# Layer 0's increments of x gathered in 128 columns, a ring of 20 KB instead of 28 KB, and 8 KB more of K kept for layer 1

## The chip, the core and the metric

One NeuronCore of one Trainium2 chip runs the whole program. Five engines work side by side and meet at semaphores: TensorE (PE, with its weight loads shown apart as PEld), VectorE (DVE), ScalarE (ACT), GpSimd (POOL) and SyncE (SP), which here only issues the DMAs. The data comes from HBM over 16 DMA engines. The metric is the device time of one execution in microseconds (us), the median of the runs. "KB" below is always KB for each of the 128 partitions: 1 KB is 256 float32 numbers of a row, and 128 KB of memory over all partitions.

## The reference

Two layers of a decoder for four sequences with one token each, in float32. x has shape 4 x 512. Both layers use the same weights and the same cache.

```python
def _A_ref(x, k_cache, v_cache, wq, wo):       # 32 query heads, 8 heads of K and V, 4096 positions, Dh 128
    q = (x @ wq).reshape(B, Sq, Hq, Dh).transpose(0, 2, 1, 3)
    scores = jnp.einsum("bhqd,bhkd->bhqk", q, k) * (Dh ** -0.5)
    o = jnp.einsum("bhqk,bhkd->bhqd", _softmax(scores), v)
    return o.transpose(0, 2, 1, 3).reshape(B, Sq, Hq * Dh) @ wo

def _B_ref(x, w1, w3, w2):                     # 512 -> 1792 -> 512
    h = _silu(x @ w1) * (x @ w3)
    return h @ w2

x = x + _A_ref(_layernorm(x), k_cache, v_cache, wq, wo)
x = x + _B_ref(_layernorm(x), w1, w3, w2)
x = x + _A_ref(_layernorm(x), k_cache, v_cache, wq, wo)
x = x + _B_ref(_layernorm(x), w1, w3, w2)
```

K and V hold 64 KB for each of the 8 heads of K and V, wq and wo 64 KB each, w1, w3 and w2 28 KB each.

## The kernel before

**Memory.** One tile, `arena`, of 218 KB is handed out by the program itself. `WQ` (0 to 64) holds wq for all heads, `WO` (64 to 128) first takes K and V of layer 0 and then wo, `KEPT` (128 to 192) at the end of layer 0 holds V of the last head (`TURN`, head 7), which layer 1 uses first. From 192 to 216 lies the ring of the transition between the layers, `PT` (214, 2 KB) is the turned softmax weights, `FIRST` (216, 2 KB) holds a piece of K.

**The list of loads.** `plan` is a list of all loads in the order in which they are issued. `pump()` goes through it and issues each load on SP's queue as soon as a place is free; it stops at the first that has none. `done` and `vacate` give a place back behind the last instruction that reads it, and call `pump` again. SP carries the list out in order: a load whose place is still being read holds up all loads behind it. With `at` a load goes to a given place, otherwise `take` looks for the lowest free one.

**The order of work.** Layer 0 goes through heads 0 to 7, layer 1 through 7 to 0. For each head, `scores` multiplies q with 8 blocks of K (8 KB each), `factors`, `exponents` and `turn_p` make the softmax weights, and `weigh` multiplies with V of the head before. After head 7 of layer 0 comes the transition: `project_o` for all 8 heads, `collect` (adds the increment to x), `feed_forward` of layer 0 (w1, w3, w2), `collect` again, `project_q` of layer 1, and `scores` of head 7.

**The ring.** In the transition 84 KB of w1, w3 and w2 and the first pieces of layer 1's K pass through 7 places of 4 KB: the first 4 KB of `WO` (its part of wo is kept in PSUM meanwhile, `stash` and `restore`) and 24 KB from 192. The pieces are w1a, w3a (4 KB, 4 of each: the first 256 of each 448 columns), w1b, w3b (3 KB, 4 of each), w2 (4 KB, 7), and seven halves of K blocks (4 KB). `feed_forward` uses them in the order w1a, w3a, w1b, w3b 0 and 1, w2 0 (`down(0)`), w3b 2 and 3, w2 1 to 6; L124 to L140 list the loads in that same order.

**What is kept of K.** While layer 0 scores the first block of head 7, ACT copies 2 KB of it to PSUM (`keptk`, L417) and POOL 2 KB to `first` (L418). Layer 1 begins its scores with these (L406), so the first half block need not be loaded again. Blocks 0 to 3 (`SPLIT`) of head 7 come to layer 1 in halves, blocks 4 to 7 whole (8 KB).

**The increments of x.** `whole` and `pair` (L484 to L496) multiply with 512 or 256 columns; the four parts of the sum lie in 32-row groups of `x_ps` over all 512 columns. `collect` copies them to SBUF (DVE 256 columns, ACT 256), adds the four groups and turns them to 128 rows with four products against `rows` (L335), and adds the mean with one more (L338). `idle` and `busy` are products without use, which keep TensorE at work.

**Layer 1's q.** `q_product` (L348) multiplies with the 8 KB of wq of one head and gives them back with `vacate`; the next whole K blocks of layer 1 are loaded there.

Of the kernel before, what the change touches and what calls it, by code (L numbers as in the profile page):

```python
# [10 lines left out]
ALU = mybir.AluOpType  # L11
# [3 lines left out]
LAYERS = 2  # L15
# [18 lines left out]
SPLIT = 4  # L34
# [4 lines left out]
def tile_decode_layers(ctx: ExitStack, tc: tile.TileContext, x, kt, v, wq, wo, w1, w3, w2, w2s, out):  # L39
# [12 lines left out]
    PT, FIRST = ARENA - 4, ARENA - 2  # L52
    free = [(WO, PT - WO)]
    ring = {"to": 0}

    def take(n, at=None):
        if at is not None and at < WO:
            return at
        for i, (lo, size) in enumerate(free):
            if at is None and state["next"] > ring["to"]:  # L60

                end = min(lo + size, PT)
                if lo < WO + 4 and end > WO:
                    if WO - lo >= n:
                        end = WO
                    else:
                        lo = WO + 4
                if end - lo < n:
                    continue
                a = lo  # L70
                lo, size = free[i]
            else:
                a = lo if at is None else at
            if lo <= a and a + n <= lo + size:
                free[i:i + 1] = [(p, s) for p, s in ((lo, a - lo), (a + n, lo + size - a - n)) if s]
                return a
        return None
# [46 lines left out]
    RING = KEPT + 64  # L124
    slots = [WO] + [RING + 4 * i for i in (5, 4, 3, 2, 1, 0)]
    for i in range(4):
        piece("w1a", i, (slots[6], slots[1], slots[2], slots[3])[i])
    for i in range(4):
        piece("w3a", i, (slots[4], slots[5], slots[0], slots[6])[i])
    for i in range(4):  # L130
        piece("w1b", i, RING + 21 - 3 * i)
# [140 lines left out]
    first = arena[:, FIRST * KB:]  # L272
    pT = arena[:, PT * KB:FIRST * KB].rearrange("p (i r) -> p i r", i=NI)
# [51 lines left out]

    def collect():
# [14 lines left out]

        def mean():
            m = misc()
            nc.tensor.matmul(m[:, 0, :], both.broadcast_to([P, P]), off[:, 0, :], start=True, stop=True)  # L344
            nc.vector.tensor_tensor(mu, mu, m[:, 0, :], op=ALU.subtract)
        return mean

    def q_product(layer, g, ps, j, first, last):  # L348
        w = loaded("wq", 0, g).rearrange("p (k n) -> p k n", k=KC)
        lo = PAD - B * j  # L350
        for k in range(KC):
            nc.tensor.matmul(ps[32 * k:32 * k + 32, :], xpad[:, 32 * k + lo:32 * k + lo + 32], w[:, k, :], start=first, stop=last)  # L352
        if layer:
            vacate("wq", 0, g)
# [45 lines left out]
    def scores(layer, g, pieces=iter(())):  # L400
        for blk in range(NB):
            split = layer == 1 and g == TURN and blk < SPLIT
            keys = [("half", layer, 2 * blk + i) for i in range(2)] if split else [("k", layer, g, blk)]
            if split and blk == 0:
                for b, k in enumerate((p, first)):
                    nc.tensor.matmul(s_ps[32 * b:32 * b + 32, :], qpad[:, 32 * b + PAD:32 * b + PAD + 32], k, start=True, stop=False)  # L406
                del keys[0]
            lo = PAD - REP * blk
            for i, key in enumerate(keys):
# [6 lines left out]
            if g == TURN and blk == 0 and not layer:  # L416
                nc.scalar.copy(keptk, loaded(*keys[0])[:, 0:BK])  # L417
                nc.gpsimd.tensor_copy(first, loaded(*keys[0])[:, BK:2 * BK])  # L418
            for key in keys:
                done(*key)  # L420
# [71 lines left out]
    def whole(i, left, w, first):  # L492

        for n in range(2):
            r = 32 * (2 * i + n)
            nc.tensor.matmul(x_ps[r:r + B, :], left(2 * i + n), w(n), start=first, stop=False)  # L496
# [10 lines left out]
    def project_o(layer, g, first=False, last=False):  # L507
        for i in range(2):
# [3 lines left out]
            if last:  # L512
                pair(i, lambda h: oT(layer, g)[:, h, :], lambda j: w[:, j, :], False, last and i == 1)
            else:
                whole(i, lambda h: oT(layer, g)[:, h, :], lambda j: w[:, j, :], first)
# [5 lines left out]
    def feed_forward(layer, mean):  # L521
# [32 lines left out]
        def columns(rows, m, w, last=False):  # L554
            for k in range(KC):
                nc.tensor.matmul(x_ps[32 * k:32 * k + B, 0:P], hT[rows, m, :], w[rows, k * P:(k + 1) * P],  # L556
                                 start=False, stop=last)

        def few(lo, hi):
            for u in range(lo, hi):  # L560
                at = (where["few"] + 2 * u) * KB
                columns(slice(0, FEW), WT + u, arena[:, at:at + 2 * KB])
# [51 lines left out]
        for m in range(1, WT):  # L614
            columns(slice(0, P), m, loaded("w2", layer, m), m == WT - 1)
# [10 lines left out]
    for layer in range(LAYERS):  # L626
# [38 lines left out]
        feed_forward(layer, collect())  # L665
        if layer < LAYERS - 1:
            mean = collect()
# [43 lines left out]
```

## Time and profile before

| | |
|---|---|
| median of 3 runs | 705.38 us (705.28 to 705.43) |
| the profiled execution | 705.23 us, its span 703.4 us, so 1.8 us lie around the span |
| TensorE clock granted | 0.808 of full speed on average |
| busy: PE, DVE, ACT, POOL | 409.9, 85.2, 38.0 and 3.5 us |
| read from HBM | 298.33 MB, 424 GB/s over the span |
| transition, first o product to first score product of layer 1 | 344.98 to 390.12 us |

A group of instructions stands on one row with its line, engine, operation, tiles written and read, and count; "x8" of a matrix product in float32 is four products, since each is made of two instructions. In the timeline the first column is the start, the second the time up to the end of the group, and the brackets tell the idle time before it and what ended it. The DMA rows give the busy share of the 16 DMA engines in tenths and the GB/s in equal slices.

### The profile page before, as it was taken

The numbers are of one execution on the slowest core, as the hardware profiler recorded it, in microseconds if no ns is written. First come the engines' busy times: TensorE is split into PE (matmuls) and PEld (weight loads), VectorE is DVE, ScalarE is ACT, GpSimd is POOL, SyncE is SP. The second block draws the span as 40 slices with busy tenths as digits, with TensorE's granted clock in tenths as the row PEclk, the third lists the DMA queues.
The fourth block names the chain that finished last, engine by engine and source line by source line (L and its number), as shares of the span: only waits on it lengthen the run. The fifth ranks groups of instructions, "written<-read, shape, count | busy, mean of one in ns | idle before, by whom it ended". The sixth has DMA issues, their size and how long they took to land. (4 is left out here: it accounts for less than half of the span.)

```text
span 703.4 us, 7079 instructions
## 1 busy us (share of the span) xinstructions
PE 409.9 (58%) x3172; PEld 136.4 (19%) x3172; DVE 85.2 (12%) x291; ACT 38.0 (5%) x87; POOL 3.5 (0%) x11
## 2 busy tenths in 40 slices
PE   2555454456456454538888894365563545467687
PEld 1112011112111111112233331011120111122234
DVE  2001010101001010101111111020000101010111
ACT  0000000000000000101001000000000000000100
POOL 0000000000000000000000000000000000000000
PEclk9986776767777776878999997588787878688899
DMA  9999999999999999999999999999999999999996
GB/s 418 432 403 466 422 418 426 462 415 432 433 444 418 440 444 421 421 428 427 414 404 403 420 431 461 429 425 418 459 425 425 437 444 418 432 433 420 424 424 277
DMA packets 13605, 298.85 MB, mean 425 GB/s; under 512 B 1655, under 2 KB 1783, under 8 KB 6263
## 3 DMA queue, kind: packets, MB, share of 16 engines
q1 hardware_dynamic: 13440, 298.39, 99.1%
q8 instruction: 25, 0.41, 0.2%
q14 instruction: 5, 0.04, 0.0%
q10 hardware_dynamic: 135, 0.01, 0.0%
HBM read 298.33 MB, written 0.07 MB: 424 GB/s over the span
## 5 line engine op out<-in xcount | busy, mean ns | idle before, releaser
L461 PE MATMUL o_ps<-arena 128*32 128x512 f32 x1024 | 146.8, 723 | 144.4 <-DMA arena<-in_v 131.0
L414 PE MATMUL s_ps<-arena,qpad 128*32 128x512 f32 x1020 | 150.1, 742 | 90.1 <-DMA arena<-in_kt 90.1
L461 PEld LDWEIGHTS o_ps<-arena 128*32 128x32 f32 x1024 | 37.4, 130 | 251.9 <-issue 222.4
L414 PEld LDWEIGHTS s_ps<-arena,qpad 128*32 128x32 f32 x1020 | 39.5, 132 | 183.7 <-issue 176.6
L470 DVE SCALAR_TENSOR_TENSOR p<-o_ps,parts,p 128x512 f32<-128x512 f32 x16 | 12.0, 751 | 266.9 <-PE o_ps L461 266.9
L424 DVE TENSOR_REDUCE top<-s_ps 128x1 f32<-128x512 f32 x16 | 11.1, 691 | 196.9 <-PE s_ps L414 196.9
L468 ACT ACTIVATE p<-o_ps,parts 128x512 f32<-128x512 f32 x16 | 11.0, 687 | 189.9 <-PE o_ps L461 182.3
L292 PE MATMUL m_ps<-ident,rows 128*32 128x256 f32 (+1 forms) x84 | 20.9, 352 | 0.0
L352 PE MATMUL o_ps<-arena,xpad 128*32 128x512 f32 x112 | 15.4, 672 | 7.9 <-DMA arena<-in_wq 7.9
L447 PE MATMUL t_ps<-ident,p 128*128 128x128 f32 x64 | 11.4, 305 | 13.5 <-ACT p L441 13.5
L474 PE MATMUL t_ps<-ident,p 128*128 128x128 f32 x64 | 10.5, 287 | 13.9 <-DVE p L470 13.8
L496 PE MATMUL x_ps<-arena,qT 128*4 128x512 f32 x112 | 13.8, 592 | 5.4 <-DVE qT L482 3.6
L434 ACT ACTIVATE f<-d 128x1 f32<-128x1 f32 x16 | 3.2, 203 | 252.8 <-DVE d L432 252.8
L441 ACT ACTIVATE p<-s_ps,top 128x512 f32<-128x512 f32 x16 | 10.9, 684 | 77.3 <-PE t_ps L474 77.3
L448 DVE COPY arena<-t_ps 128x512 f32<-128x512 f32 x16 | 11.1, 691 | 9.7 <-PE t_ps L447 9.7
L474 PEld LDWEIGHTS t_ps<-ident,p 128*128 128x128 f32 x64 | 6.7, 140 | 28.2 <-DVE p L470 28.2
L447 PEld LDWEIGHTS t_ps<-ident,p 128*128 128x128 f32 x64 | 7.3, 150 | 22.2 <-ACT p L441 19.2
L292 PEld LDWEIGHTS m_ps<-ident,rows 128*32 128x32 f32 x84 | 9.0, 110 | 9.0 <-issue 3.5
L529 PE MATMUL o_ps<-arena,xpad 128*32 128x192 f32 (+1 forms) x128 | 8.1, 360 | 1.0 <-DMA arena<-in_w 0.9
L529 PE MATMUL s_ps<-arena,xpad 128*32 128x192 f32 (+1 forms) x128 | 7.9, 359 | 1.3 <-DMA arena<-in_w 1.3
L489 PE MATMUL x_ps<-arena,qT 128*4 128x256 f32 x88 | 6.6, 379 | 2.4 <-DMA arena<-in_w 1.7
L352 PEld LDWEIGHTS o_ps<-arena,xpad 128*32 128x32 f32 x112 | 3.6, 121 | 17.2 <-DMA arena<-in_wq 8.8
(107 smaller groups left out, 144.2 us busy)
## 6 DMA issues: line engine op xcount, KB each, us to landing
arena<-in_v SPq DMA_DIRECT2D x4, 4096.0 KB, 38.4
arena<-in_w SPq DMA_DIRECT2D x17, 512.0 KB, 13.4
arena<-in_kt SPq DMA_DIRECT2D x8, 1024.0 KB, 11.3
arena<-in_kt SPq DMA_DIRECT2D x2, 4096.0 KB, 18.1
arena<-in_wq SPq DMA_DIRECT2D x1, 7168.0 KB, 39.8
arena<-in_v SPq DMA_DIRECT2D x3, 2048.0 KB, 31.8
arena<-in_wo SPq DMA_DIRECT2D x1, 4096.0 KB
arena<-in_kt SPq DMA_DIRECT2D x2, 2048.0 KB
```

Source lines behind the costliest of these rows:

```text
L292: nc.tensor.matmul(m_ps[0:32, (4 - w) * P:], rows, ident.unsqueeze(1).broadcast_to([P, w, P]), start=True, stop=True)
L352: nc.tensor.matmul(ps[32 * k:32 * k + 32, :], xpad[:, 32 * k + lo:32 * k + lo + 32], w[:, k, :], start=first, stop=last)
L414: nc.tensor.matmul(s_ps[32 * b:32 * b + 32, :], qpad[:, 32 * b + lo:32 * b + lo + 32], k[:, j, :], start=(blk == 0), stop=(blk == NB - 1))
L424: nc.vector.tensor_reduce(top[:, 0:1], s_ps, axis=AX.X, op=ALU.max, negate=True)
L447: nc.tensor.transpose(t_ps[:, i, :], p[:, i * P:(i + 1) * P], ident)
L448: nc.vector.tensor_copy(pT.rearrange("p i r -> p (i r)"), t_ps.rearrange("p i r -> p (i r)"))
L461: nc.tensor.matmul(o_ps[32 * b:32 * b + 32, :], pT[:, i, 32 * b:32 * b + 32], w[:, b, :], start=(i == 0), stop=(i == NI - 1))
L468: nc.scalar.activation(p, o_ps, AF.Copy, scale=st["parts"][:, 0:1])
L470: nc.vector.scalar_tensor_tensor(p, o_ps, st["parts"][:, 1:2], p, op0=ALU.mult, op1=ALU.add)
L474: nc.tensor.transpose(t_ps[:, j, :], p[:, j * P:(j + 1) * P], ident)
L496: nc.tensor.matmul(x_ps[r:r + B, :], left(2 * i + n), w(n), start=first, stop=False)
L529: nc.tensor.matmul(ps[32 * j:32 * j + 32, lo:lo + n], x32[:, k, :], w[:, j * n:(j + 1) * n], start=(k == 0), stop=(k == KC - 1))
```

## The change

It touches three things. (1) K: besides the 4 KB of before, POOL copies the rest of block 0 and half of block 1 (`more_k`, 8 KB at 192) in layer 0, and layer 1 scores six parts from copies (`held`) before it needs a load. `SPLIT` becomes 5, so block 4 comes in halves too. (2) The ring: 192 to 200 is taken by `more_k`, the ring has 16 KB from 200 and the 4 KB of `WO`, 5 places, each used in turn. The loads are listed plainly: w1a, w3a, w1b, w3b, w2 and the halves 3 to 7; halves 8 and 9 go to the first 8 KB of wq that layer 1's q has read, which `q_product` now gives back in two parts. (3) x in layer 0: the last head's o product and the last two pieces of w2 are made of products with 128 columns (`columns`), the sum of the pieces before is copied and folded in by four products (`fold`), and `gather` takes the place of `collect`: one DVE operation over 128 columns and one product against the unit matrix.

```diff
-SPLIT = 4
+SPLIT = 5
+MKB = 8
-    PT, FIRST = ARENA - 4, ARENA - 2
-    free = [(WO, PT - WO)]
+    PT, FIRST, MORE = ARENA - 4, ARENA - 2, KEPT + 64
+    free = [(WO, MORE - WO), (MORE + MKB, PT - MORE - MKB)]
-        if at is not None and at < WO:
+        if at is not None and at < WO and state["next"] < 4:
             return at
...
-    RING = KEPT + 64
-    slots = [WO] + [RING + 4 * i for i in (5, 4, 3, 2, 1, 0)]
...
-    for i in range(2):
-        piece("w3b", i, RING + 9 - 3 * i)
-    piece("w2", 0, slots[0])
-    for i in range(2, 4):
-        piece("w3b", i, RING + 9 - 3 * i)
-    for i in range(1, 7):
-        piece("w2", i, slots[i])
-    for i in range(7):
-        piece("half", i + 1, slots[i])
+    RING = MORE + MKB
+    slots = [WO] + [a for a in range(FIRST - 4, RING - 1, -4)]
+    turns = [len(slots) - 1, *range(1, len(slots) - 1), 0]
+    pieces = [(name, i) for name, n in (("w1a", KC), ("w3a", KC), ("w1b", KC), ("w3b", KC), ("w2", WT // 2)) for i in range(n)]
+    pieces += [("half", i) for i in range(1 + MKB // 4, 2 * SPLIT - 2)]
+    for n, (name, i) in enumerate(pieces):
+        piece(name, i, slots[turns[n % len(turns)]])
+    for i in range(2):
+        piece("half", 2 * SPLIT - 2 + i, WQ + 8 * TURN + 4 * i)
...
+    def gather(ps):
+        both = small("both")
+        nc.vector.scalar_tensor_tensor(p[:, 0:P], ps[:, 0:P], 1.0, unit.broadcast_to([P, P]), op0=ALU.mult, op1=ALU.mult,
+                                       accum_out=both)
+        m = misc()
+        idle(2)
+        nc.tensor.matmul(flat(m), p[:, 0:P], ident.rearrange("p (k c) -> p k c", k=KC)[:, :, 0:B], start=True, stop=False)
+        nc.tensor.matmul(flat(m), both.broadcast_to([P, P]), flat(off), start=False, stop=True)
+        idle(1)
+        nc.vector.tensor_tensor(xc, xc, m, op=ALU.add)
+        return total_of(both)
+
+    def fold(ps, to, first):
+        nc.vector.tensor_copy(p, ps)
+        for k in range(KC):
+            nc.tensor.matmul(to[32 * k:32 * k + B, 0:P], rows[:, 0:B], chunk(k), start=first, stop=False)
...
+        if layer and first and last:
+            for f in range(2):
+                for k in range(KC):
+                    nc.tensor.matmul(ps[32 * k:32 * k + 32, 256 * f:256 * f + 256], xpad[:, 32 * k + lo:32 * k + lo + 32],
+                                     w[:, k, f, :], start=True, stop=True)
+                give(where["wq", 0, g][0] + 4 * f, 4)
+                pump()
+            return
...
+            n = len(held) - B * blk
+            if split and n > 0:
+                for b, k in enumerate(held[B * blk:B * blk + B]):
+                    nc.tensor.matmul(s_ps[32 * b:32 * b + 32, :], qpad[:, 32 * b + lo:32 * b + lo + 32], k, start=(blk == 0), stop=False)
+                del keys[:n // 2]
+                if n <= B:
+                    give(MORE, MKB)
+                    pump()
...
         def down(i):
             ws = [loaded("w2", layer, 2 * i + n) for n in range(2)]
-            pair(i, lambda m: hT[:, m, :], lambda n: ws[n], i == 0, i == WT // 2 - 1)
             for n in range(2):
-                done("w2", layer, 2 * i + n)
-            busy((1, 2, 2, 2, 1, 2, 0)[i])
+                m = 2 * i + n
+                if i < 5:
+                    nc.tensor.matmul(x_ps[32 * (m % 4):32 * (m % 4) + B, :], hT[:, m, :], ws[n], start=(m < 4), stop=(m > 5))
+                else:
+                    columns(s_ps, hT[:, m, :], ws[n], m == 10, m == WT - 1)
+                done("w2", layer, m)
+            if i == 5:
+                fold(x_ps, s_ps, False)
+            busy((1, 1, 1, 1, 1, 1, 0)[i])
```

The order in which `feed_forward` uses the pieces (L593 to L596) is not part of the diff: `down(0)` still stands between w3b 1 and w3b 2. The host lays wq out so that each head's 8 KB are two halves of 256 columns.

More of the change, by code (lines that the diff above doesn't have):

```diff
@@ L272, in tile_decode_layers @@
     first = arena[:, FIRST * KB:]
+    more_k = arena[:, MORE * KB:(MORE + MKB) * KB]
+    held = [p, first] + [more_k[:, i * BK:(i + 1) * BK] for i in range(MKB // 2)]
     pT = arena[:, PT * KB:FIRST * KB].rearrange("p (i r) -> p i r", i=NI)
@@ L403, in scores @@
             keys = [("half", layer, 2 * blk + i) for i in range(2)] if split else [("k", layer, g, blk)]
[L404 to L407, printed above, removed]
             lo = PAD - REP * blk
+            n = len(held) - B * blk
[6 more added lines that the diff above has]
+                    pump()
             for i, key in enumerate(keys):
@@ L418, in scores @@
                 nc.gpsimd.tensor_copy(first, loaded(*keys[0])[:, BK:2 * BK])
+            if g == TURN and not layer:
+                lo, hi = max(2, B * blk), min(len(held), B * blk + B)
+                if hi > lo:
+                    nc.gpsimd.tensor_copy(more_k[:, (lo - 2) * BK:(hi - 2) * BK],
+                                          loaded(*keys[0])[:, (lo - B * blk) * BK:(hi - B * blk) * BK])
             for key in keys:
@@ L490, in pair, with whole @@
                                  start=first, stop=last)
-    def whole(i, left, w, first):
+    def whole(ps, i, left, w, first, last):
         for n in range(2):
-            r = 32 * (2 * i + n)
-            nc.tensor.matmul(x_ps[r:r + B, :], left(2 * i + n), w(n), start=first, stop=False)
+            r = 32 * ((2 * i + n) % 4)
+            nc.tensor.matmul(ps[r:r + B, :], left(2 * i + n), w(n), start=first, stop=last)
     def stash():
@@ L507, in project_o @@
     def project_o(layer, g, first=False, last=False):
+        left = oT(layer, g)
         for i in range(2):
@@ L511, in project_o @@
             w = loaded(*key).rearrange("p (h e) -> p h e", e=D)
-            if last:
-                pair(i, lambda h: oT(layer, g)[:, h, :], lambda j: w[:, j, :], False, last and i == 1)
-            else:
-                whole(i, lambda h: oT(layer, g)[:, h, :], lambda j: w[:, j, :], first)
+            if last and layer:
+                pair(i, lambda h: left[:, h, :], lambda j: w[:, j, :], False, i == 1)
+            elif last:
+                for j in range(2):
+                    columns(x_ps, left[:, 2 * i + j, :], w[:, j, :], i + j == 0, i + j == 2)
+                if i == 0:
+                    fold(s_ps, x_ps, False)
+            else:
+                whole(x_ps if layer else s_ps, i, lambda h: left[:, h, :], lambda j: w[:, j, :], first,
+                      not layer and g == TURN - 1)
             if layer or n == 0:
@@ L561, in few @@
                 at = (where["few"] + 2 * u) * KB
-                columns(slice(0, FEW), WT + u, arena[:, at:at + 2 * KB])
+                columns(x_ps, hT[0:FEW, WT + u, :], arena[0:FEW, at:at + 2 * KB])
         sq = squares()
@@ L614, in feed_forward @@
         for m in range(1, WT):
-            columns(slice(0, P), m, loaded("w2", layer, m), m == WT - 1)
+            columns(x_ps, hT[:, m, :], loaded("w2", layer, m), False, m == WT - 1)
             done("w2", layer, m)
@@ L664, in tile_decode_layers @@
             project_o(layer, before[0], False, True)
-        feed_forward(layer, collect())
-        if layer < LAYERS - 1:
-            mean = collect()
+        feed_forward(layer, collect() if layer else gather(x_ps))
+        if not layer:
+            mean = gather(s_ps)
     y = p[:, 0:P]
```

31 lines of the change are left out of this document (13 added, 18 removed).

## The prediction

> **What bounds the kernel now.** I read the page first: how much of the span the DMA engines are busy, and with what.
>
> ```profile
> span 703.4 us, 7079 instructions
> PE 409.9 (58%) x3172; PEld 136.4 (19%) x3172; DVE 85.2 (12%) x291; ACT 38.0 (5%) x87; POOL 3.5 (0%) x11
> ...
> DMA  9999999999999999999999999999999999999996
> GB/s 418 432 403 466 422 418 426 462 415 432 433 444 418 440 444 421 421 428 427 414 404 403 420 431 461 429 425 418 459 425 425 437 444 418 432 433 420 424 424 277
> ...
> q1 hardware_dynamic: 13440, 298.39, 99.1%
> q8 instruction: 25, 0.41, 0.2%
> ```
>
> SP's queue (q1) keeps the 16 DMA engines busy for 99.1% of the span; only the last slice has a hole. No compute engine comes near that. So bytes set the time, and a microsecond in which no DMA engine has work is lost for good, while an idle or slow PE costs nothing as long as places come free in time. The next view is the table of windows, for the price of a byte.
>
> ```profile
> 350.00:360.00 10.00, 9.49 (x86) 3.63 (x79) 0.94 (x5) 0.47 (x2) 0.00 (x0) 1.00 1.02 408
> 361.50:366.00 4.50, 4.03 (x42) 1.62 (x42) 0.72 (x3) 0.47 (x1) 0.55 (x1) 1.00 1.03 405
> 383.00:387.00 4.00, 4.00 (x35) 2.26 (x38) 1.17 (x7) 0.85 (x3) 0.34 (x1) 1.00 1.03 412
> 391.00:403.00 12.00, 10.98 (x100) 3.49 (x92) 1.59 (x4) 0.37 (x1) 0.00 (x0) 1.00 1.01 419
> 560.00:600.00 40.00, 22.27 (x158) 6.59 (x154) 4.19 (x13) 1.67 (x4) 0.00 (x0) 0.80 1.02 440
> ```
>
> The last two columns are the DMA share and GB/s. The share is full in the transition too (a little over 1 by the way it is counted), so the old ring of 7 places never runs dry. The rate falls with the length of a row: 440 GB/s with rows of 64 KB, 419 with 8 KB, 412 and 408 with 4 KB, 405 with 3 and 4 KB mixed.
>
> **The bytes.** Before, 7 half blocks and 4 whole blocks of head 7's K are loaded for layer 1: 60 KB for each partition. After, halves 3 to 9 and 3 blocks: 52 KB. 8 KB x 128 = 1.05 MB are gone. As rows of 4 KB at 412 GB/s they took 2.55 us; block 4, now in halves, costs 1.05 MB x (1/412 - 1/419) = 0.04 us more. **Term: -2.5 us.**
>
> **The ring.** Here the bytes could be given back. The timeline of TensorE shows how w3b and w2 are used:
>
> ```profile
> 370.12 0.53 PE L529 MATMUL o_ps<-arena,xpad 128*32 128x192 f32 x8
> ...
> 371.04 0.53 PE L529 MATMUL o_ps<-arena,xpad 128*32 128x192 f32 x8 [0.19 <-DMA arena<-in_w]
> 371.39 0.59 PE L292 MATMUL m_ps<-ident,rows 128*32 128x256 f32 x2
> 372.41 0.61 PE L489 MATMUL x_ps<-arena,qT 128*4 128x256 f32 x8 [0.42 <-DMA arena<-in_w]
> 372.84 0.38 PE L292 MATMUL m_ps<-ident,rows 128*32 128x128 f32 x2
> 373.28 0.53 PE L529 MATMUL o_ps<-arena,xpad 128*32 128x192 f32 x8
> 373.63 0.38 PE L292 MATMUL m_ps<-ident,rows 128*32 128x128 f32 x2
> 374.25 0.53 PE L529 MATMUL o_ps<-arena,xpad 128*32 128x192 f32 x8 [0.24 <-DMA arena<-in_w]
> 374.60 0.38 PE L292 MATMUL m_ps<-ident,rows 128*32 128x128 f32 x2
> 375.59 0.61 PE L489 MATMUL x_ps<-arena,qT 128*4 128x256 f32 x8 [0.61 <-DMA arena<-in_w]
> ...
> 376.79 0.61 PE L489 MATMUL x_ps<-arena,qT 128*4 128x256 f32 x8 [0.16 <-DMA arena<-in_w]
> ```
>
> L529 is a piece of w3b, L489 a piece of w2, L292 filling. PE waits for each piece and uses them as they come, 0.97 us apart for 3 KB (373.28 to 374.25), 1.28 for 4 KB (0.52 MB at 408 GB/s): w3b 0, 1, w2 0, w3b 2, 3, w2 1, 2. The new list loads w3b 0 to 3 first and w2 0 behind them, while `feed_forward` still calls `down(0)` after w3b 1. What a refill takes:
>
> ```profile
> 374.85 0.33 SPq L182 DMA_DIRECT2D arena<-in_w  x1
> ```
>
> w3b 3 starts at 374.25, ends 0.53 later at 374.78, and SP issues into its place at 374.85: 0.07 us. Issue to first byte, at the start of the program (second row: busy tenths of the DMA in slices of 0.1 us from 0.5):
>
> ```profile
> 0.73 0.38 SPq L182 DMA_DIRECT2D arena<-in_wq  x1
> ...
> DMA  0000000000009909920049929979979998996998
> ```
>
> Issued at 0.73, first bytes in the thirteenth slice, 1.7 to 1.8: about 1.0 us. The Trainium skill ("DMA: Bandwidth & Descriptors", Specifications) gives some 0.6 us to the first byte for this path; the trace disagrees by 0.4 us and decides; by the page the hole worked out below would be 0.4 us smaller. Last byte to PE, at the end of the program (slices of 0.225 us from 692):
>
> ```profile
> DMA  9999999799989837686868767455521300000000
> ...
> 699.97 0.40 PE L556 MATMUL x_ps<-arena,qT 128*4 128x128 f32 x8
> ```
>
> The last busy slice ends at 692 + 32 x 0.225 = 699.2 to 699.4; PE starts at 699.97: I take 0.54 us.
>
> An ordinary step then fits into 5 places. From the moment a 3 KB piece is ready to the moment the next one in its place is ready: 0.53 + 0.07 + 1.0 + 0.97 + 0.54 = 3.11 us, and the other pieces give 5 x 0.97 = 4.85 us; slack 1.7. With 4 KB pieces (0.64 for the product, at 360.08 below): 3.53 against 6.4, slack 2.9.
>
> The mixed order doesn't fit. The bytes ahead are the same, so w2 0, fifth in the new order, is ready when the fifth of the old was: 374.25. Until then PE stands before `down(0)`, and w3b 2 and 3 lie in their places unused. Places go round in fives, so w2 3 needs that of w3b 2, and the two loads between, w2 1 and 2, are all that the DMA has left. Their last byte lands 0.54 before 376.79: 376.25. `down(0)` now multiplies with 512 columns:
>
> ```profile
> 352.40 1.04 PE L496 MATMUL x_ps<-arena,qT 128*4 128x512 f32 x8 [0.19 <-DMA arena<-in_wo]
> ...
> 353.26 0.38 PE L292 MATMUL m_ps<-ident,rows 128*32 128x256 f32 x1
> ```
>
> The next product starts 0.86 us after the first. So: 374.25 + 0.86 (`down(0)`) + 0.2 (the filling product, an estimate: half of the pace of the 256-column ones) + 0.53 (w3b 2) + 0.07 + 1.0 = 376.91. The engines stand from 376.25 to 376.91. **Term: +0.7 us** (nothing, if a refill is that much quicker under load; 1.2 if the filling and the restart of 16 engines cost more, the bytes at the start needing 0.5 us to come to full rate).
>
> Before and after this place I find slack. The first refill: after the last wo piece (used from 354.96) five pieces of 1.28 us keep the DMA until about 360.8, and
>
> ```profile
> 354.96 0.61 PE L489 MATMUL x_ps<-arena,qT 128*4 128x256 f32 x8 [0.17 <-DMA arena<-in_wo]
> ...
> 357.74 1.70 PE L529 MATMUL s_ps<-arena,xpad 128*32 128x256 f32 x24
> ...
> 358.44 1.39 SPq L182 DMA_DIRECT2D arena<-in_w  x3
> ...
> 360.08 0.64 PE L529 MATMUL s_ps<-arena,xpad 128*32 128x256 f32 x8 [0.23 <-DMA arena<-in_w]
> ```
>
> SP issued at 358.44, so first bytes by 359.5 even without a quicker `gather`. After the hole PE comes to w2 1 late, by about 1 us, and needs 1.07 us for each piece against 1.28 for a load: w2 3 to 6 and halves 3 to 7 keep over 1 us each by the same sum; half 8 waits for the first half of q's product and has 1.7 us.
>
> **The lead of the faster engines.** The slices from 692 on fall from 9 to 1 over 5 us: the 16 engines don't finish together. When the ring runs dry, all wait for the same issue, and those ahead lose their lead; what makes them differ later (25 instruction loads, 0.2% of 16 x 703.4 us or some 0.9 us each, on one engine at a time) adds up anew. That costs nothing if the engine that is last at 377 us is also last at the end, and up to one such pause, 0.9 us, if it is another. I can't tell which from this view and take the nearer end: **+0.3 us**. The Trainium skill ("DMA: Bandwidth & Descriptors", Why a DMA increments its semaphore by 16 and not by 1) says that the engines finish independently and only the full count means landed; the slices agree.
>
> **What lies beside.** The two new POOL copies (4 x 512 columns) stand before the release of head 7's K blocks in layer 0:
>
> ```profile
> 294.99 0.61 POOL L418 COPY arena<-arena 128x512 f32<-128x512 f32 x1 [284.45 <-DMA arena<-in_kt]
> ...
> 300.58 3.63 SPq L182 DMA_DIRECT2D arena<-in_v  x4
> ```
>
> 5 x 0.61 from 294.99 is 298.0, and SP can issue only at 300.58, when PE has done four blocks: hidden by 2.5 us; without that cover it would take from the DMA's backlog, not from its time. The rest:
>
> ```profile
> 381.87 0.61 PE L489 MATMUL x_ps<-arena,qT 128*4 128x256 f32 x8 [0.24 <-DMA arena<-in_w]
> 382.55 0.42 DVE L329 SCALAR_TENSOR_TENSOR p<-x_ps,few 128x256 f32<-128x256 f32 x1 [2.70 <-PE x_ps L489]
> ...
> 383.02 0.38 ACT L331 ACTIVATE p<-x_ps 128x256 f32<-128x256 f32 x1 [11.40 <-DVE p L329]
> ...
> 384.65 1.07 PE L352 MATMUL t_ps<-arena,xpad 128*32 128x512 f32 x8
> ```
>
> ```profile
> L448 DVE COPY arena<-t_ps 128x512 f32<-128x512 f32 x16 | 11.1, 691 | 9.7 <-PE t_ps L447 9.7
> ```
>
> From the last piece of w2 to q it is 2.8 us now. `gather` drops the ACT step and three of five products, some 0.9 us by estimate; `fold` adds a DVE copy (0.69 us for 512 columns by L448's mean) and eight instructions beside the last two pieces. Since PE starts late, I get q's product between 0.9 us earlier and 0.4 later. The DMA has some 8 KB in its queue then: **nothing** either way. q's product in two parts gives its place back earlier by half. Layer 1's later loads find the same places.
>
> **Sum.** 705.23 (profiled: span 703.4 and 1.8 around it) - 2.5 + 0.7 + 0.3 = 703.7. The median shown is 0.15 above the profiled execution, so 703.9.
>
> **Rivals.** (a) *No hole, or half of it*: refills into a running queue are quicker than the first of the program. For it: 16 engines never paused in the old ring. Against: the order alone leaves the DMA two loads for some 2.7 us of work. Then only the bytes count: 705.4 - 2.5 = 702.9 to 703.2. By the Trainium skill's 0.6 us (the section above) the hole would be 0.3 and the time 703.2. (b) *The lead costs in full*, or the hole is 1.2: 705.4 - 2.5 + 0.7 + 0.9 = 704.5, and 704.1 to 704.9 around it, which can't be told from no change. (c) *More holes*: half 8, the first refill or a late `fold` lose their slack, 0.5 to 1 us each: 704.5 to 705.5. (d) *Slower*: the first byte takes much longer in mid-run than at the start, and the ring's rounds become longer than its loads. Every microsecond beyond 1.0 goes into the hole in full; beyond 2.7 the eight 3 KB pieces, 1.6 rounds of five places, lose the excess each round too. It takes the 2.5 us back from 2.8, and from 3.3 (hole 3.0, rounds 0.9) the kernel is slower by over 1.4: 706.8 and above. Against it: 1.0 us in the queue's own row; for it: no row shows an issue into a short queue in mid-run. (e) *The change doesn't save the bytes*: the list shows 7 + 3 loads in place of 7 + 4, so only a slip in my count would do this: 705.4 or more.
>
> **How the numbers follow.** A measurement of this kernel tells about 0.2%, 1.4 us, from no change: faster means below 703.97. The forecast, hole with little or no loss of lead (703.5 to 704.2): 0.42, about two thirds of it below the line. (a) 0.20, (b) 0.18, (c) 0.13, (d) 0.05, (e) 0.02. Faster 0.28 + 0.20 + a little of (b) = 0.51; same 0.14 + 0.15 + 0.12 + 0.02 = 0.43; slower 0.06. From 702.7 to 705.3 leaves out (d), (e) and the end of (c).
>
> **What would show it.** Right: 297.3 MB read; the old place before `down(0)` with PE waiting about 3 us for w2 0; the DMA share well under 1 between 374 and 377, at most some 0.7 us of it with no byte at all; full share elsewhere up to the last 6 us. Wrong: full share there (a), holes at 358 to 360 or 385 to 389 (c), a hole every 5 us (d), or a hole of the right size and an end that lies later than the sum by up to 1 us with a steeper fall in the last slices (b).

## The result and the profile after

Five timed runs of the changed kernel had a median of 709.35 us, five of the kernel before 705.28 us; the ratio of changed to before is 1.0076, with a 95% interval of 1.0047 to 1.0106. The forecast was 703.9 us, 702.7 to 705.3. The kernel became slower by 4.1 us between the medians and by 5.4 us by the ratio, which goes by all executions (two of the five took 711.2 and 713.9 us), where it was expected to be faster by 1.4. Every ratio below is taken against the kernel before on the same chip, and 0.0010 of it is 0.7 us. One execution of 803 us, in the first run with six places, was far longer than the other nine and is left out of that run's ratio and median.

The page of the changed kernel, its profiled execution taking 709.30 us; "DMA" and "GB/s" are the span in 40 slices:

```profile
span 707.5 us, 7130 instructions
...
DMA  9999999999999999999998999999999999999996
GB/s 415 430 401 471 416 419 460 419 427 456 416 433 438 426 438 430 431 421 426 410 360 295 418 436 449 432 416 459 426 416 449 433 415 449 434 411 429 422 427 275
...
q1 hardware_dynamic: 13296, 297.34, 98.5%
...
HBM read 297.28 MB, written 0.07 MB: 420 GB/s over the span
...
arena<-in_w SPq DMA_DIRECT2D x8, 384.0 KB, 4.8
```

Two things can be read at once. The bytes went as forecast: 1.05 MB fewer on q1 (298.39 before). And the loss lies in two slices, the 21st and 22nd (354 to 389 us), with 360 and 295 GB/s where 404 and 403 stood. The last row is that of the 3 KB pieces: from issue to landing 4.8 us in the middle. Before:

```profile
arena<-in_w SPq DMA_DIRECT2D x8, 384.0 KB, 7.5
```

A load that lands 7.5 us after its issue had much queued ahead of it. 4.8 us is about the time that the five places themselves hold at full rate (5 x 0.97). The windows of the changed kernel, by stage and then closer (the last two columns are the DMA share and GB/s, the one ahead of them the granted clock):

```profile
350.00:375.00 25.00, 19.07 (x218) 8.09 (x210) 3.31 (x13) 2.38 (x4) 0.56 (x1) 0.99 0.97 361
375.00:400.00 25.00, 23.22 (x209) 9.84 (x213) 3.18 (x14) 0.96 (x2) 0.55 (x1) 0.87 0.91 345
...
358.00:360.00 2.00, 1.21 (x14) 0.38 (x10) 0.00 (x0) 0.00 (x0) 0.00 (x0) 1.00 0.86 297
...
366.00:368.00 2.00, 1.13 (x19) 0.66 (x19) 0.31 (x1) 0.00 (x0) 0.00 (x0) 1.00 0.99 336
...
374.00:376.00 2.00, 0.27 (x2) 0.13 (x4) 0.00 (x0) 0.00 (x0) 0.00 (x0) 0.67 0.88 328
376.00:378.00 2.00, 2.00 (x13) 0.72 (x10) 0.00 (x0) 0.00 (x0) 0.00 (x0) 0.50 0.58 236
378.00:380.00 2.00, 2.00 (x24) 1.38 (x20) 0.19 (x1) 0.00 (x0) 0.00 (x0) 0.50 0.28 37
380.00:382.00 2.00, 2.00 (x13) 0.66 (x7) 0.23 (x1) 0.00 (x0) 0.00 (x0) 0.63 0.82 301
```

The same two stages before moved 404 and 412 GB/s, and the row from 366 had 397:

```profile
350.00:375.00 25.00, 22.07 (x230) 9.48 (x223) 3.06 (x14) 2.85 (x6) 0.55 (x1) 1.00 1.02 404
375.00:400.00 25.00, 23.47 (x213) 9.61 (x217) 3.10 (x16) 1.80 (x5) 0.55 (x1) 1.00 1.02 412
...
366.00:368.00 2.00, 1.70 (x22) 0.78 (x20) 0.40 (x1) 0.00 (x0) 0.00 (x0) 1.00 1.04 397
```

So 25 x (404 - 361)/404 = 2.7 us and 25 x (412 - 345)/412 = 4.1 us of DMA time went unused, 6.7 in all, against 2.5 us of bytes saved; the difference, 4.2, is what lies between the two profiled executions (709.30 and 705.23). The hole that the prediction placed at 376 us is there and is the largest piece: from 376 to 382, 3.2 us at 408 GB/s are missing where 0.7 were forecast. But about half of the loss lies elsewhere: at the first refill (0.86 and 297 GB/s in the row from 358, although SP issued at 357.58), and from 366 to 376, where no row has a hole (336 GB/s at a share of 0.99 in the first, 328 at 0.88 in the last).

```profile
357.58 0.33 SPq L175 DMA_DIRECT2D arena<-in_w  x1
```

How can a share near 1 go with a low rate? The packets in the trace tell it. w1b and w3b come as 1024 packets of 3 KB. The middle one takes 0.12 us in both kernels, but in the changed one 5.3% of them take over 0.2 us and hold 16% of the packets' time, against 0.3% and 0.7% before. A slow packet counts as busy.

The timeline of TensorE and of SP's queue in the changed kernel at the hole (start, time, instruction, and in brackets the wait ahead of it):

```profile
371.62 0.53 PE L571 MATMUL o_ps<-arena,xpad 128*32 128x192 f32 x8 [0.23 <-DMA arena<-in_w]
...
375.73 1.88 PE L594 MATMUL x_ps<-arena,qT 128*4 128x512 f32 x4 [3.16 <-DMA arena<-in_w]
...
377.71 0.94 PE L571 MATMUL o_ps<-arena,xpad 128*32 128x192 f32 x5
...
378.74 0.33 SPq L175 DMA_DIRECT2D arena<-in_w  x1
```

The DMA share there, in slices of 0.2 us from 374:

```profile
DMA  5867997999999666431004000000996268998999
```

PE waits 3.16 us for w2 0, as forecast, but w2 0 comes at 375.73 and not at 374.25, and `down(0)` then takes 1.88 us. The engines run out one after another from 376.6 to 377.8 (digits 6 to 1), and the next bytes of the ring come at 379.6, 0.9 us behind the issue at 378.74 (the 4 at 378.2 is a single packet of the instruction queue). During PE's wait its granted clock fell to half, some 2.1 us after the last product (0.67 in the row from 374), and it stayed there until 381.5 (0.50 from 376 to 380), so everything up to that issue took nearly twice its time. The Trainium skill ("TensorE: Matmul & The Clock Gate", Part 1: The HAM clock gate) says that PE falls back to half of its clock after an idle window of about 3.4 us; the trace agrees only in part: the wait was 3.16 us long, but the clock fell 2.1 us into it. In one run below it fell half a microsecond behind a wait of 2.14 us and in another it stayed at 1.00 over one of 2.44 us, so the length of the wait alone doesn't decide.

### The profile page after: what moved, and what is told of

It reads as the page before. It is cut to its first block, busy times and chain, and to the rows that moved or that the text cites. A ratio compares the mean times of both kernels' runs of the same rounds, so it can differ in the third digit from the quotient of the medians.

```text
span 707.5 us, 7130 instructions
## 1 busy us (share of the span) xinstructions
PE 408.2 (58%) x3196; PEld 136.5 (19%) x3196; DVE 85.9 (12%) x291; ACT 37.0 (5%) x83; POOL 5.5 (1%) x13
## 3 DMA queue, kind: packets, MB, share of 16 engines
HBM read 297.28 MB, written 0.07 MB: 420 GB/s over the span
## 5 line engine op out<-in xcount | busy, mean ns | idle before, releaser
L496 PE MATMUL o_ps<-arena 128*32 128x512 f32 x1024 | 144.6, 713 | 147.2 <-DMA arena<-in_v 133.8
L444 PE MATMUL s_ps<-arena,qpad 128*32 128x512 f32 x1012 | 147.6, 738 | 89.4 <-DMA arena<-in_kt 89.4
L531 PE MATMUL s_ps<-arena,qT 128*4 128x512 f32 x56 | 6.6, 592 | 3.1 <-DMA arena<-in_wo 3.1
```

The lines of the kernel that those rows point to most:

```text
L496: nc.tensor.matmul(o_ps[32 * b:32 * b + 32, :], pT[:, i, 32 * b:32 * b + 32], w[:, b, :], start=(i == 0), stop=(i == NI - 1))
L531: nc.tensor.matmul(ps[r:r + B, :], left(2 * i + n), w(n), start=first, stop=last)
```

## The experiments

The theories at the start. **Places**: with fewer places, and with places that come free in another order than the loads, too little is queued while PE works; the DMA engines that are ahead run dry first, and all of their lost time counts. **The hole**: one hole at `down(0)`, lengthened by the clock, is the whole loss, and the rest is as predicted.

**The order alone.** The changed kernel, with w2 0 listed where it is used:

```
+    pieces.insert(3 * KC + 2, pieces.pop(4 * KC))
```

> The changed kernel with one line more: w2 0 is listed between w3b 1 and w3b 2, as feed_forward uses it. Theory A (the order: PE stands 3 us before down(0), its clock falls to half, the place of w3b 2 comes free late and the DMA has a hole from 377.3 to 380): PE's wait of 3.2 us and the clock of 0.5 are gone, no slice of the transition without bytes, 703 to 704.2 us. Rival B (five places are too few in any order, since the faster of the 16 DMA engines run dry): the rate between 366 and 376 us stays at 320 to 350 GB/s and 2 us or more stay lost, 705 to 707.5.

Measured: ratio 1.0036 (1.0023 to 1.0049), median 708.02 us. That is slower than either theory expected. PE's wait, the half clock and the hole behind `down(0)` are gone, and 0.0040, 2.8 us, with them. But the rates stay low:

```profile
350.00:375.00 25.00, 20.86 (x233) 8.73 (x233) 3.32 (x13) 2.38 (x4) 0.55 (x1) 1.00 0.99 371
375.00:400.00 25.00, 22.15 (x223) 8.70 (x219) 3.56 (x15) 0.96 (x2) 0.55 (x1) 1.00 1.00 385
```

With a share of 0.99 and 1.00, 371 and 385 GB/s cost 2.0 and 1.6 us against before. One dip is left, at the first refill (0.83 and 289 GB/s from 358 to 360); the rest of the loss has no hole. Five places are too few in the order of use too.

**The clock alone.** Twelve filling products keep PE busy before `down(0)`:

```
         if keep:
+            busy(12)
             down(0)
```

> The changed kernel, its order as it is, with filling products (12 times 128 columns, some 2.7 us) ahead of down(0), so that TensorE doesn't stand. Theory A with the clock as a part of its own: the granted clock stays at 1.0 between 374 and 382, down(0) takes 1.0 us in place of 1.9, the place of w3b 2 is free 1.3 us earlier, and the time falls by 1.3 to 2.3 to 707 to 708. If the wait alone counts and not the clock: no change, 709.3. Rival B: no change.

Measured: ratio 1.0063 (1.0043 to 1.0084), median 710.81 us: no gain that can be told (four executions; the interval overlaps that of the changed kernel). The clock stayed at 1.00 up to 384 us and the issue came 2.0 us earlier:

```profile
375.07 1.03 PE L594 MATMUL x_ps<-arena,qT 128*4 128x512 f32 x4 [0.45 <-DMA arena<-in_w]
...
376.71 0.33 SPq L175 DMA_DIRECT2D arena<-in_w  x1
...
380.10 0.60 PE L594 MATMUL x_ps<-arena,qT 128*4 128x512 f32 x2 [1.10 <-DMA arena<-in_w]
...
383.79 0.60 PE L594 MATMUL x_ps<-arena,qT 128*4 128x512 f32 x2 [2.14 <-DMA arena<-in_w]
```

Yet PE waits 1.10 and 2.14 us for the pieces that follow, and the stage moved fewer bytes than the 345 GB/s of the changed kernel, as its window shows:

```profile
375.00:400.00 25.00, 21.68 (x208) 9.45 (x212) 3.18 (x14) 0.96 (x2) 0.55 (x1) 0.93 0.93 327
```

The hole from 376 to 382 us is still there, if smaller: 227 GB/s in place of 191, where the kernel before moved 395. So the half clock made the hole longer, but without it the loss went to other places: by the same sum as above the two stages lose 7.3 us here (370 and 327 GB/s) and 6.7 in the changed kernel.

**The bytes alone.** The kernel before without half blocks 1 and 2:

```
-    for i in range(7):
+    for i in range(2, 7):
         piece("half", i + 1, slots[i])
...
```

The scores of the two parts are made with K that is kept, so this kernel leaves a part of the computation out.

> The kernel before, its ring of 7 places untouched, without the loads of the half blocks 1 and 2 (8 KB); the scores of these parts are made with the kept piece instead, so this part of the result is wrong. It measures the term of the bytes alone: 1.05 MB at 412 GB/s, 2.55 us, so 702.7 by every theory; if it is 704 or more, the bytes weren't worth what the prediction took, and the loss in the ring is smaller by as much.

Measured: ratio 0.9999 (0.9989 to 1.0010), median 705.63 us. It reads the same 297.28 MB as the changed kernel and gains nothing, where every theory expected 2.5 us or so. Its windows:

```profile
375.00:400.00 25.00, 23.59 (x218) 9.40 (x211) 3.20 (x15) 1.80 (x5) 0.55 (x1) 1.00 1.00 385
```

385 in place of 412 GB/s is 1.6 us of the 2.5; no single window shows where the rest went. SP's queue shows why, by its first half block:

```profile
377.96 0.33 SPq L182 DMA_DIRECT2D arena<-in_kt  x1
```

The kernel before issues its first one here:

```profile
375.23 0.42 SPq L182 DMA_DIRECT2D arena<-in_kt  x1
```

The two halves that were left out were the two that could be issued early. Without them SP's first half block goes out 2.7 us later, while the queue runs low.

**Seven places with the plain list.** The changed kernel with no K kept, so all bytes and all places of before:

```
-MKB = 8
+MKB = 0
...
-                if n <= B:
+                if n <= B and MKB:
```

> The changed kernel with MKB = 0: no more K kept than before (so the same bytes as before), ring of 7 places, but the plain list of loads and the new x sums. Theory A says that the wrong order needs the short ring to hurt: PE still stands 3 us before down(0) and its clock still falls, but four loads, 5.1 us, lie between and the hole is under 0.5 us: 705.0 to 706.0. If the order alone were to blame for all of it, 709 or more. Rival B: 705.3.

Measured: ratio 1.0040 (1.0025 to 1.0054), median 708.34 us. No theory had this: with seven places too the time is 2.8 us longer, and without the clock's help. PE's wait for w2 0 on the timeline:

```profile
374.93 1.03 PE L594 MATMUL x_ps<-arena,qT 128*4 128x512 f32 x4 [2.44 <-DMA arena<-in_w]
```

The windows behind it, with the clock at 1.00 and the rate at 342 and 303 GB/s:

```profile
376.00:378.00 2.00, 2.00 (x32) 1.23 (x25) 0.42 (x1) 0.00 (x0) 0.00 (x0) 1.00 0.96 342
...
380.00:382.00 2.00, 1.71 (x26) 0.68 (x22) 0.73 (x2) 0.00 (x0) 0.00 (x0) 1.00 0.89 303
```

**Seven places in the order of use.** The two edits together (order and no K kept) leave, beside the gathering of x's increments, three smaller differences from before: q is made in two products, block 4 of K comes in halves, and the pieces of 3 KB lie in places of 4 KB, where the kernel before has them side by side, eight in 24 KB.

> The changed kernel with none of the 8 KB of K kept (so a ring of 7 places and all the bytes of before) and with w2 0 listed between w3b 1 and w3b 2; the gathering of x's increments stays. Theory (the number of places and the order of the places bind, the gathering costs nothing): PE's wait ahead of the first w2 product is gone, the ring is that of before, and the time is that of before, 705.4 to 706.2, so that the 2.5 us of the run with 7 places and the plain list were the order's. Rival (the gathering itself costs: the fold, the extra columns and the later running sum lengthen the chain that frees the places): 707 to 708, with the dips of the DMA share still there at 376 to 390.

Measured: ratio 1.0002 (0.9993 to 1.0012), median 705.32 us. All of these together cost and bring nothing that can be told, and the 2.7 us between this run and the last are the order's.

**Six places.** The order of use and half of the K:

```
-MKB = 8
+MKB = 4
...
```

> The changed kernel with 4 KB of K kept in place of 8 (ring of 6 places, 0.52 MB fewer than before) and with w2 0 listed between w3b 1 and w3b 2. Theory (each place taken from the ring costs more than the 1.25 us that its bytes save): between the runs with 7 and 5 places in that order, 706.3 to 707.3. Rival (a threshold: 5 places are too few, 6 are enough, and the saved bytes then count): 704.0 to 705.0.

Measured: ratio 1.0012 (1.0001 to 1.0023), median 705.77 us of nine. 0.52 MB fewer, and no gain: the ratio lies between theory and rival. The rate fell only in the stage of w1 and w3, from 364 to 372 us, where pieces of 3 KB lie in places of 4 (the windows of its second run, below).

**The same bytes saved, with a full queue.** The kernel before with its seven places, where the seven early loads are halves 3 to 9 and one block of K fewer follows:

```
-SPLIT = 4
+SPLIT = 5
...
-        piece("half", i + 1, slots[i])
+        piece("half", i + 3, slots[i])
...
```

Here too the scores of the parts left out are made with K that is kept.

> The kernel before with its ring of 7 places, where the seven half blocks that follow w2 are the 3rd to the 9th in place of the 1st to the 7th and the next whole block of K is left out: 8 KB a partition (1.05 MB) fewer are loaded and as many early loads stand in the queue as before. The scores of block 0 and of the first half of block 1 of that head are made with K that is already kept, so these scores are of other keys. Theory (bytes count where the queue stays full; the earlier run with the same bytes gained nothing because two early loads were missing): 2.0 to 2.5 us less than before, 702.9 to 703.6 beside a kernel before of 705.4. Rival (the end is set by something other than the bytes, so no loading less helps): within 0.7 us of before.

Measured: ratio 0.9967 (0.9955 to 0.9979), median 702.95 us. This is the run that separates the theories: the same 1.05 MB that brought nothing before bring 2.3 us as soon as as many loads stand in the queue as before. With w1 and w3 at the old 404 GB/s the queue runs low only behind w2 (its profiled execution, 703.95 us, is the slowest of its six):

```profile
350.00:375.00 25.00, 21.95 (x230) 9.48 (x222) 3.04 (x14) 2.85 (x6) 0.55 (x1) 1.00 1.02 404
375.00:400.00 25.00, 22.25 (x201) 8.49 (x201) 3.07 (x15) 1.80 (x5) 0.55 (x1) 1.00 1.01 394
```

**What a ring can carry, by itself.** Behind the output of the kernel before, loads of 4 KB a partition go round in rings of 1, 2, 3 and 5 places; a copy of 0.29 us on VectorE reads each place and frees it:

```
+    for places, loads in ((1, 6), (2, 12), (3, 18), (5, 30)):
+        for i in range(loads + places):
+            if i >= places:
+                at = 4 * (i % places) * KB
+                nc.vector.tensor_copy(p[:, 256:512], arena[:, at:at + 256])
+            if i < loads:
+                at, lo = 4 * (i % places) * KB, 4 * (i % 7) * KB
+                nc.sync.dma_start(arena[:, at:at + 4 * KB], w1[:, lo:lo + 4 * KB])
```

> The kernel before with a measurement behind the output: four chains of loads of 4 KB a partition into rings of 1, 2, 3 and 5 places (6, 12, 18 and 30 loads), each place read by one copy on VectorE and then loaded again; the results are thrown away and the time is longer by the chains. Theory of the prediction (0.07 us from free to issue, 1.0 us to the first byte, 1.28 us of bytes, 0.54 us to the reader, about 0.2 us of copy): 3.1 us a load with one place, 1.55 with two, 1.28 (the DMA's full rate) with three and five. Theory of the result (the engines start and end a load at different times, and one that ran dry restarts slowly): 3.3 to 3.8 us with one place, 1.7 to 1.9 with two, 1.35 to 1.5 with three, 1.28 with five only.

Measured, in one execution and in windows that hold the turns of each ring without its start:

```profile
706.18:721.60 15.42, 0.00 (x0) 0.00 (x0) 1.17 (x4) 0.00 (x0) 0.00 (x0) 0.50 0.45 136
729.59:750.26 20.67, 0.00 (x0) 0.00 (x0) 2.64 (x9) 0.00 (x0) 0.00 (x0) 0.50 0.71 220
757.19:788.19 31.00, 0.00 (x0) 0.00 (x0) 4.70 (x16) 0.00 (x0) 0.00 (x0) 0.50 0.84 280
791.08:823.99 32.91, 0.00 (x0) 0.00 (x0) 7.05 (x24) 0.00 (x0) 0.00 (x0) 0.50 1.00 392
```

One turn with one place takes 15.42 / 4 = 3.86 us, not the 3.1 that the prediction's pieces make. Three places, which 3 x 1.28 = 3.84 would nearly fill, run at 280 GB/s, 1.87 us a load, and two at 220, 2.38 us; both theories expected less for each of these. One turn in slices of 0.1 us from 706, issued at 706.18:

```profile
DMA  0000000000088999007889899988842100000000
GB/s 0 0 0 0 0 0 0 0 0 0 0 164 205 205 205 287 41 41 246 246 328 369 328 410 410 451 369 328 328 164 82 41 0 0 0 0 0 0 0 0
```

and the reader of this turn on the timeline:

```profile
709.74 0.29 DVE L675 COPY p<-arena 128x256 f32<-128x256 f32 x1 [3.58 <-DMA arena<-in_w]
```

The first bytes come in the slice from 707.1, 0.95 us behind the issue (1.0 was taken). The reader starts 0.5 us behind the last ones, at 709.2 (0.54 was taken). It is the load itself that differs: 2.1 us for bytes that a full queue moves in 1.28. The engines are busy (8 and 9) and move half of their rate in the first half microsecond; the two slices of 0 behind it are no pause, since the view counts a packet in the slice in which it starts. The packets themselves show it: of the 26 of 4 KB that begin in that first half microsecond the middle one takes 0.33 us and the longest 0.70, while all 63 that begin after 708.3 take 0.16. At the end some engines are done sooner than others.

**Rings of 4 places, and of 3 KB.** The same measurement with 4 places of 4 KB, then 5, 6 and 7 of 3 KB.

```
+    for places, loads, n in ((4, 24, 4), (5, 30, 3), (6, 30, 3), (7, 35, 3)):
...
```

> The kernel before with chains behind the output as in the first measurement of rings (whose rates were 136, 220, 280 and 392 GB/s with 1, 2, 3 and 5 places of 4 KB): now 4 places of 4 KB (24 loads), then 5, 6 and 7 places of 3 KB (30, 30 and 35 loads), each read by one copy and loaded again; the results are thrown away. Theory (one turn takes 3.86 us with one place, and the engines' unequal speed makes a ring need more places than that turn divided by the bytes' time): 340 to 365 GB/s with 4 places of 4 KB, 330 to 370 with 5 of 3 KB, 370 to 400 with 6, the full 390 to 410 with 7. Rival (one turn alone counts: 3.86 us over 4 places, 3.54 us over 5 are under the 1.28 and 0.96 us of the bytes): 390 to 410 GB/s in all four.

Measured, again in one execution:

```profile
707.59:734.61 27.02, 0.00 (x0) 0.00 (x0) 5.59 (x19) 0.00 (x0) 0.00 (x0) 0.50 1.00 371
740.87:767.16 26.29, 0.00 (x0) 0.00 (x0) 7.05 (x24) 0.00 (x0) 0.00 (x0) 0.50 0.99 358
773.94:797.40 23.46, 0.00 (x0) 0.00 (x0) 6.76 (x23) 0.00 (x0) 0.00 (x0) 0.50 1.02 387
799.36:830.72 31.36, 0.00 (x0) 0.00 (x0) 9.41 (x32) 0.00 (x0) 0.00 (x0) 0.50 1.03 401
```

Five places of 3 KB lose 11% against seven (358 and 401 GB/s) even with a reader that takes 0.29 us and waits for nothing else. Three of the four lie where the theory had them; four places of 4 KB, 371, a little above.

**A reader that is late.** The ring of 5 and of 7 places of 4 KB once more; a place is read and freed only when the load behind it, or the second behind it, has landed too:

```
+    for places, loads, late in ((5, 30, 1), (5, 30, 2), (7, 35, 1), (7, 35, 2)):
...
+                for j in (min(i - places + late, loads - 1), i - places):
...
```

> The kernel before with chains behind the output: rings of 5 and 7 places of 4 KB (30 and 35 loads) in which a place is read, and loaded again, only when the load behind it (late by 1) or the second behind it (late by 2) has landed too; the results are thrown away. It stands for a reader that takes the pieces in another order than they come. Theory (being late by one costs a place): 5 places late by 1 run as 4 (340 to 365 GB/s), late by 2 as 3 (270 to 290); 7 places run as 6 and as 5, 385 to 410 in both. Rival (a ring of 5 has room for it): within 5% of the 392 GB/s of 5 places in all four.

Measured, in one execution and in the order of the list:

```profile
707.93:743.01 35.08, 0.00 (x0) 0.00 (x0) 14.10 (x48) 0.00 (x0) 0.00 (x0) 0.50 0.99 354
753.90:797.58 43.68, 0.00 (x0) 0.00 (x0) 14.11 (x48) 0.00 (x0) 0.00 (x0) 0.50 0.86 283
806.76:842.47 35.71, 0.00 (x0) 0.00 (x0) 15.87 (x54) 0.00 (x0) 0.00 (x0) 0.50 1.02 407
854.81:889.25 34.44, 0.00 (x0) 0.00 (x0) 15.88 (x54) 0.00 (x0) 0.00 (x0) 0.50 1.01 395
```

Late by one, five places run about as four do (354 and 371 GB/s), late by two as three do (283 and 280). Seven have room for both (407 and 395). The plain list makes the reader late in this way: w2 0 is needed before w3b 2 and 3, which lie in their places in the meantime. But lateness alone isn't all of it: a bare ring of seven hardly feels it, while in the kernel the plain list with seven places cost 2.7 us. What the chain leaves out is that PE stands 2.44 us there and then works off what has piled up; no run parts the two.

**A denser ring of 24 KB.** Six places again, but the pieces of 3 KB side by side, so that seven of them fit; beside it the run with six places once more:

```
...
+    at = [0, 16, 12, 8, 4, None, 0, 16] + [13, 10, 7, 4, None, 0, 16, 13, 10] + [4, None, 0, 16, 12, 8] + [4, None, 0, 16, 12, 8]
+    for (name, i), a in zip(pieces, at, strict=True):
+        piece(name, i, WO if a is None else RING + a)
```

> As the run with 6 places, 4 KB of K kept and w2 0 between w3b 1 and w3b 2, but the pieces of 3 KB (w1b, w3b) lie side by side in the 24 KB, so that seven of them are held where six were. Theory (what that run lost, it lost at 360 to 375 us, where pieces of 3 KB stood in places of 4 KB and the rate was 361 to 392 GB/s; 388 against 404 GB/s over 350 to 375 is 1.0 us): the rate there comes back to about 400 GB/s and the time falls by 0.7 to 1.0 us against that run, to 704.4 to 705.2 beside a kernel before of 705.4: the half of the bytes' saving that fits beside a full queue. Rival (six places are too few wherever the pieces lie, or the loss lies elsewhere): no change against that run, 705.7 to 706.4.

> The run with 6 places, 4 KB of K kept and w2 0 between w3b 1 and w3b 2 once more, so that it stands beside the packed one on the same chip. Its ten times spread from 704.9 to 708.1 about a median of 706.2; by the rates in its trace it should lose 1.0 us and save 1.2, 705.2 to 706.2. Rival: 706.5 and above, as the plain share of the loss between 7 and 5 places would give.

Measured: ratio 1.0004 (0.9995 to 1.0013), median 705.52 us, for the dense ring; 1.0008 (0.9998 to 1.0018), median 706.46 us, for the other, between its forecast and its rival. The windows of the dense one:

```profile
350.00:375.00 25.00, 21.65 (x244) 9.34 (x244) 3.31 (x13) 2.38 (x4) 0.56 (x1) 1.00 1.02 398
375.00:400.00 25.00, 23.77 (x230) 9.38 (x227) 3.90 (x16) 1.33 (x3) 0.55 (x1) 1.00 1.02 405
```

and of the other:

```profile
350.00:375.00 25.00, 21.49 (x236) 8.98 (x234) 3.31 (x13) 2.38 (x4) 0.55 (x1) 1.00 1.01 386
375.00:400.00 25.00, 23.45 (x225) 8.95 (x225) 3.60 (x15) 1.33 (x3) 0.55 (x1) 1.00 1.02 414
```

The rate in w1 and w3 came back (386 to 398), as expected, but 9 GB/s went in the stage behind it, and the forecast of 704.4 to 705.2 was missed. Whether the two differ at all can't be told: their intervals overlap. What can be told is that neither shows a gain over the kernel before, though both load 0.52 MB less; no version tried here with the whole computation in place does.

## Why the prediction was wrong

The runs part the 0.0076 by which the kernel became slower as follows; the parts are taken as differences, so they add up by themselves. The bytes, with a full queue: -0.0033 (-2.3 us). The order: 0.0040 (2.8 us, give or take 2.2) between the changed kernel and its run in the order of use, 0.0038 (2.7 us, give or take 1.2) between the two with seven places; these are two separate measurements of it. The gathering: 0.0002. What remains is the two places less: the run with five places in the order of use stands 0.0034 above the one with seven, and has 0.0033 of bytes to its credit, so they cost 0.0067 (4.7 us). This last figure is a difference and was not measured by itself; from the intervals that it is made of, some 1.4 us either way is an estimate.

Point by point, by the prediction's steps:

- **The bytes, -2.5 us: right in size**, with a condition that the prediction didn't state. They count where the queue stays full (2.3 us), and not where it doesn't (nothing, in the kernel before without its first two halves).
- **The ring, +0.7 us: this is the step that failed.** Its place and its cause were right: PE stands about 3 us before `down(0)`, w3b 2 is used late, w2 3 is issued late. Its size, and the sentence that an ordinary step "fits into 5 places" with 1.7 and 2.9 us of slack, were wrong: order and places together cost 7.5 us, and w2 0 itself came at 375.73 in place of 374.25, since the ring had lost time before.
- Why the slack wasn't there. The sum of a refill took the load's own time as that of a full queue, 0.97 or 1.28 us. A load into an empty queue takes 2.1, and a turn 3.86 where the prediction's pieces give 3.1. The second error is larger: a ring was taken to run full as soon as one turn is shorter than the places' bytes. By that three places of 4 KB should be all but full, and they run at 280 GB/s; five of 3 KB, with 1.3 us to spare by the measured turn (3.86 less 0.32 us of bytes, against 5 x 0.97), run at 358. One reading of this: what a fast engine has already loaded lies in its place until the slowest engine has loaded its part and the piece has been used, so the fast engines have fewer places than the count says. An engine that has run dry then begins with slow packets, as the first half microsecond of the bare turn shows. That reading fits the slow packets from 360 to 378 us and the digits that fall from 6 to 1 one by one; no view shows the engines singly, and which was ahead by how much was not varied in any run.
- **The lead of the faster engines, +0.3 us.** The prediction saw it in the last 5 us of the span, and held that it "costs nothing if the engine that is last at 377 us is also last at the end". It looked only at the piece as PE sees it, that is at the slowest engine. By the reading above each engine's idle time counts all through the transition, and the faster ones idle first; how much of the loss is theirs was not measured, and no run parts the 0.3 us from the rest.
- **The clock**, half from 374.7 to 381.5 us, stood in no step. It nearly doubled the time from w2 0 to the next issue (3.0 us from 375.73 to 378.74, for the 1.66 that the prediction's pieces give and the 1.64 measured at full clock), and yet keeping it up brought nothing that can be told, since PE then waited for the next pieces.
- **"The first refill has slack": wrong.** It was issued at 357.58, before the 358.44 of the old kernel, and the share still fell to 0.86 in the row from 358.
- **The gathering, the fold, q in two parts: nothing. Right**, by the run at 1.0002. That run makes no further copies of K on POOL; in the changed kernel these end at 297.45, 3.6 us before SP issues into the places of that head's K (301.05), so they held nothing up, as predicted.
- **Two readings.** In the slices from 692 the last busy one ends at 699.2, not at 699.4, so that view gives up to 0.77 us from last byte to PE; the 0.54 that was taken is what the bare turn shows (709.2 to 709.74).
- **Rivals.** The slower one had the right sign and the wrong mechanism: the first byte takes 0.9 us in the hole and 0.95 in the bare turn, no more than at the start, and the bytes behind it are what is slow. The rival with more holes named one right place, the first refill, but priced each at 0.5 to 1 us and left the steady loss out.

What stays open is why the first packets of a load into an empty queue are slow, what part of the order's cost is lateness and what part PE's standing, and why the runs with six places scatter more (704.4 to 708.4 us in one set of eleven) than those of before (704.9 to 706.4 in 23).

## What to carry to other kernels

Where the DMA bounds a kernel, room in the queue is worth as much as bytes: before room is taken from a ring to save a load, measure what the ring moves with fewer places, by a bare chain of loads behind the output, and compare that with the bytes. Take the chain's rate as an upper limit: five places of 4 KB moved 392 GB/s there, and 371 and 385 in the kernel. The sum of one turn's parts is only a lower bound on the room it needs; here even 1.7 times as much (5 places of 1.28 us for a turn of 3.86) gave 392 GB/s and not the 412 of the kernel before. And a list of loads should be in the order of use: here one piece out of its turn cost about as much as a place (2.7 us, and 4.7 for two places).

## What the runs showed of the hardware that was not expected

- A load of 0.52 MB into an empty queue moved for 2.1 us, against 1.28 in a full one; the engines were busy in the first half microsecond at 164 to 287 GB/s, with packets of up to 0.70 us where 0.16 is usual.
- With a ring and a short reader, 1, 2, 3, 4, 5 places of 4 KB moved 136, 220, 280, 371, 392 GB/s; 5, 6, 7 of 3 KB moved 358, 387, 401.
- A DMA share near 1 doesn't mean full rate: 0.99 stood beside 336 GB/s at 366 us in the changed kernel, where the kernel before moved 397. Slow packets count as busy: 5.3% of those of 3 KB took over 0.2 us, against 0.3% before.
- PE's granted clock fell to half 2.1 us into a wait of 3.16 us without any product and came back after 6.8 us; it fell half a microsecond behind a wait of 2.14 us and stayed at 1.00 over one of 2.44 us.
